# A first layer by seven products over two halves of 192 rows, in place of seven over 256 rows and four over 128

## The chip, the cores and the metric

The kernel runs on one core of one Trainium2 chip. The metric is device time in microseconds (us): the median of the runs, which is 640.2 us for the kernel before (three runs, 640.17, 640.20 and 640.79 us). A profile is one execution as the hardware profiler recorded it. Engines are called by their short names: PE (TensorE, the matrix engine), PEld (its weight loads), DVE (VectorE), ACT (ScalarE), POOL (GpSimd) and SP (SyncE, which issues most DMAs).

## What is computed

A recurrent attention block ("delta net") is followed by a two-layer network with an exact GELU. All is fp32.

```python
# q, k, v: (4 batches, 8 heads, 768 tokens, 48); beta: (4, 8, 768)
k_n = k / (norm(k) + 1e-6);  state = 0
for t in range(768):
    y[t]  = q[t] @ state
    state = state + beta[t] * outer(k_n[t], v[t] - state.T @ k_n[t])
x = y as (3072 tokens, 384)                   # 384 = 8 heads x 48
h = x @ w_in                                  # w_in:  384 x 2048
out = (0.5 * h * (1 + erf(h / sqrt(2)))) @ w_out   # w_out: 2048 x 384
```

## The kernel before, in words

The 768 tokens of each batch are cut into 12 chunks of 64 (`c` = 0 to 11). A chunk holds 4 x 64 = 256 tokens in two tiles `a` = 0, 1 of 128 tokens. Each chunk goes through the attention part and then, while the next chunk's attention is worked on, through the two layers of the network. One such stretch is called a step here. Ten steps (`c` = 2 to 11) use the fast forms of the two layers; chunks 0 and 1 use plain products (`fc1`, `fc2`), which the change leaves alone.

**First layer, `c` > 1 (`part_of_layer`, L906).** The contraction of 384 rows is three blocks of 128. Blocks 0 and 1 are treated as the two halves of a 2 x 2 block product (two token tiles, two halves of the contraction, two halves of `w_in`'s 2048 columns) and done by Winograd's seven products P1 to P7 instead of eight. The weight sums are made once (`sum_of_w_in`, L869), the sums of x once a step (`mix_x`, L878). Block 2 is done plainly, by four more products R11, R12, R21, R22. That makes eleven, each done in two blocks `b` of four matmuls 128 x 128 x 128 (L916), so 88 matmuls a step. The first block's eleven parts come before the second's. PE adds up what can be added in PSUM (tiles psX, psY, psZ, psV); ACT copies partial results to `pu` in SBUF, DVE adds the rest (L939, L947, L958, L968), ACT applies the GELU (through the helper `keep`, L902) and leaves it in `G`.

**Second layer (`second_layer`, L1032).** It has seven products again, each of eight matmuls that move 192 columns (`product_`, L859). `two` starts them in the order 1, 5, 2, 6, 4, 7, 3, and `read2` adds the results up on DVE.

**Attention around it.** Small matmuls that use 64 (or 48, or 32) rows and 64 columns of PE's array, several of them side by side in its parts: `against_state` (psK, L667), `solve` (psU, L702), `use` and `update` (psY, L732 and L743), `grams` and `queries` (psG, L414), `join_run` (psJ, L593). They come in groups of 32 to 64. `turns` (L782) transposes a finished chunk's x (L788) and one ACT copy puts it into `xT`, the moving operand of the first layer.

**What sets the order.** A plan (`emit`, L1062) sorts all steps by a due time, written in units of one chunk. DVE keeps the order of the plan, and so do those ACT instructions that pass through `keep`. The layers' matmuls on PE are tied in a line one behind the other (`behind`, L888); an attention group that is passed to `together` (L623) stands directly behind the matmul traced before it. PSUM is all given out: pool `ps` has two tiles "mlp" and two "dn" of double size, pool `small` has one "z" and one "sq". A tile's next use waits until the reads of its last use are over.

In the trace each fp32 matmul is two MATMUL records: 88 matmuls a step in ten steps are 1760 records of L916. A transpose is one record.

Of the kernel before, what the change touches and what calls it, by code (L numbers as in the profile page):

```python
# [19 lines left out]
def kernel(  # L20
# [301 lines left out]
    def sum_of_squares(u, h):  # L322

        if "both" not in ns:
            n23 = wk.tile([128, 2 * NA, H], F32, tag="n23", name="n23", bufs=1)
            ns[2], ns[3] = n23[:, 0:NA], n23[:, NA:]
            ns["both"] = n23
        if h == 0:
            u.ksq = wk.tile([128, H, D], F32, tag="ksq", name="ksq", bufs=1)
        keep(nc.scalar.activation, u.ksq[:, h], u.Kn[:, h, 0:D], ACT.Square,  # L330
             accum_out=ns[u.c][:, u.a, h:h + 1])
# [27 lines left out]
    def root(x):  # L359

        shape = list(x.shape)
        s = wk.tile(shape, F32, tag="root", name="root", bufs=1)
        r = wk.tile(shape, F32, tag="root_r", name="root_r", bufs=1)
        nc.vector.tensor_scalar(s.bitcast(U32), x.bitcast(U32), 0.5, 532487669.0,
                                op0=ALU.mult, op1=ALU.add)
        nc.vector.tensor_scalar_mul(x, x, 0.5)
        for i in range(3):
            nc.vector.reciprocal(r, s)
            nc.vector.tensor_tensor(r, r, x, op=ALU.mult)
            nc.vector.scalar_tensor_tensor(x if i == 2 else s, s, 0.5, r, ALU.mult, ALU.add)  # L370
# [204 lines left out]
    def join_run(g, ts0, ts1):  # L575
# [5 lines left out]
        for level, ts in enumerate((ts0, ts1)):  # L581
            if ts:
                if both is not None:
                    psJ = both[:, level]
                else:
                    psJ = small[0].tile([128, 512], F32, tag="sq" if level else "z", name="psJ")
                sets.append((level, ts[0] * H, psJ.rearrange("q (k n) -> q k n", n=2 * HB)))
# [120 lines left out]
    def solved(u, copy):  # L708
        u.U = wk.tile([128, H, D], F32, tag="U", name="U")
# [56 lines left out]
    def turn(u):  # L766
        if u.a == 0:
            xTs[u.c] = wk.tile([128, NM, NA * 128], F32, tag="xT", name="xT")
        xT = xTs[u.c]
        psX = sq("psX", NM, 128)  # L770
        for m in range(NM):
            cols = slice(m * 128, (m + 1) * 128)
            if u.c == 1:

                for i, part in enumerate((u.x, u.y)):
                    nc.tensor.matmul(psX[:, m, :], lhsT=part.rearrange("q h d -> q (h d)")[:, cols],
                                     rhs=ident, start=i == 0, stop=i == 1)
            else:
                nc.tensor.transpose(psX[:, m, :], u.x.rearrange("q h d -> q (h d)")[:, cols], ident)
        nc.scalar.copy(xT[:, :, u.a * 128:(u.a + 1) * 128], psX)  # L780

    def turns(us):  # L782
        c = us[0].c
        xT = xTs[c] = wk.tile([128, NM, NA * 128], F32, tag="xT", name="xT")
# [5 lines left out]
        keep(nc.scalar.copy, xT.rearrange("q m (a n) -> q a m n", n=128), psX)  # L790
# [73 lines left out]
    S1, L1 = {}, {}  # L864
# [10 lines left out]

    def of_x(c, k, a):
        return xTs[c][:, k, a * 128:(a + 1) * 128]

    def mix_x(c):
        t = more[0].tile([128, 3, 128], F32, tag="TX", name="TX")  # L880
        L1["T"] = {1: t[:, 0], 2: t[:, 1], 3: of_x(c, 0, 1), 4: t[:, 2]}
        for n, a, b in ((1, of_x(c, 0, 1), of_x(c, 0, 0)), (2, of_x(c, 1, 1), t[:, 0]),
                        (3, of_x(c, 1, 1), of_x(c, 0, 1)), (4, of_x(c, 1, 0), t[:, 1])):
            nc.vector.tensor_tensor(L1["T"][n], a, b, op=ALU.subtract)
# [21 lines left out]
    def part_of_layer(c, b, n):  # L906

        fs = slice(b * FB, (b + 1) * FB)

        def product(*args):  # L910
            behind(product_, *args)

        def product_(ps_, lhs, rhs, first):
            for i in range(FB):
                f = b * FB + i
                nc.tensor.matmul(ps_[:, i], lhsT=lhs[:, f // 2, f % 2 * 128:(f % 2 + 1) * 128],  # L916
                                 rhs=rhs, start=first and i == 0, stop=True,
                                 skip_group_check=not (first and i == 0))

        def half(k, a):  # L920
            return A[a][k][:, fs]

        def fresh(name, tag, pool):
            L1[name] = pool.tile([128, FB, 128], F32, tag=tag, name=f"ps{name}")
            return L1[name]

        if n == "P1":
            if b == 0:
                L1["pu"] = more[0].tile([128, 2, FB, 128], F32, tag="S1", name="pu")
            product(fresh("X1", "mlp", ps), block(0, 0), of_x(c, 0, 0), True)  # L930
            keep(nc.scalar.copy, L1["pu"][:, 0], L1["X1"])
        elif n == "P5":
            product(fresh("Z1", "z", small[0]), S1[1], L1["T"][1], True)
            keep(nc.scalar.copy, L1["pu"][:, 1], L1["Z1"])
            if b > 0:
                keep(nc.scalar.activation, L1["last"], L1["last"], ACT.Gelu)
        elif n == "P6":
            product(fresh("Y1", "mlp", ps), S1[2], L1["T"][2], True)
            nc.vector.tensor_tensor(L1["Y1"], L1["Y1"], L1["pu"][:, 0], op=ALU.add)  # L939
        elif n == "P2":  # L940
            product(L1["X1"], block(0, 1), of_x(c, 1, 0), False)
        elif n == "R11":
            product(L1["X1"], block(0, 2), of_x(c, 2, 0), False)
            keep(nc.scalar.activation, half(0, 0), L1["X1"], ACT.Gelu)
        elif n == "P7":
            product(L1["Y1"], S1[3], L1["T"][3], False)
            nc.vector.tensor_tensor(half(1, 1), L1["Y1"], L1["pu"][:, 0], op=ALU.add)  # L947
            keep(nc.scalar.activation, half(1, 1), half(1, 1), ACT.Gelu)
        elif n == "R22":
            product(L1["Z1"], block(1, 2), of_x(c, 2, 1), False)  # L950
            keep(nc.scalar.copy, L1["pu"][:, 0], L1["Z1"])
        elif n == "P3":
            product(fresh("V1", "sq", small[0]), S1[4], of_x(c, 1, 1), True)
        elif n == "R12":
            product(L1["V1"], block(0, 2), of_x(c, 2, 1), False)
        elif n == "P4":
            product(L1["Y1"], block(1, 1), L1["T"][4], False)
            nc.vector.tensor_tensor(half(0, 1), L1["V1"], L1["pu"][:, 1], op=ALU.add)  # L958
        else:
            product(L1["Y1"], block(1, 2), of_x(c, 2, 0), False)  # L960
            keep(nc.scalar.activation, half(1, 0), L1["Y1"], ACT.Gelu)
            L1["last"] = half(0, 1)
            if b == NB - 1:
                keep(nc.scalar.activation, L1["last"], L1["last"], ACT.Gelu)
                mix(c, 1, 1)

    def add_p5():
        nc.vector.tensor_tensor(L1["pu"][:, 1], L1["Y1"], L1["pu"][:, 1], op=ALU.add)  # L968
# [14 lines left out]
    def two(c, n):  # L983
        if n == 1:
            W2["X"] = ps.tile([128, 2, DH], F32, tag="mlp", name="psX2")
            W2["o"] = [wk.tile([128, DM], F32, tag="o_sb", name="o_sb") for a in range(NA)]
            product(W2["X"][:, 0], A[0][0], B11, True)
        elif n == 5:
            W2["Z"] = small[0].tile([128, DH], F32, tag="z", name="psZ2")
            product(W2["Z"], W2["S"], T[1], True)  # L990
            W2["p1"] = more[0].tile([128, DH], F32, tag="p1", name="p1")
            nc.scalar.copy(W2["p1"], W2["X"][:, 0])
# [9 lines left out]
        else:  # L1002
            W2["V"] = dn("psV2")[:, 0, 0:DH]
            product(W2["V"], A[0][1], B22, True)

    def read2(c, n):
        o, X, Y, Z = W2["o"], W2["X"], W2["Y"], W2["Z"]
        if n == 6:
            W2["u2"] = o[0][:, DH:]
            nc.vector.tensor_tensor(W2["u2"], Y[:, 0], W2["p1"], op=ALU.add)  # L1010
        elif n == 7:
            W2["u3"] = W2["p1"]
            nc.vector.tensor_tensor(W2["u3"], Y[:, 0], W2["p1"], op=ALU.add)
            nc.vector.tensor_tensor(o[1][:, 0:DH], X[:, 1], W2["u3"], op=ALU.add)
            nc.vector.tensor_tensor(o[1][:, DH:], Z, W2["u3"], op=ALU.add)
            tiles[c, 1].o = o[1]
            send(tiles[c, 1])
            nc.vector.tensor_tensor(W2["u2"], Z, W2["u2"], op=ALU.add)
            tiles[c, 0].o = o[0]
        else:  # L1020
            nc.vector.tensor_tensor(o[0][:, DH:], W2["V"], W2["u2"], op=ALU.add)
# [10 lines left out]
    def second_layer(c, n):  # L1032

        two(c, n)
        if n == 1:
# [5 lines left out]
    def ffn_steps(c):  # L1041
        ones = [(1.3, fc1, c, f) for f in range(NF)]
        if c > 1:
            return [(0.88, part_of_layer, c, b, n) for b in range(NB)
                    for n in ("P1", "P5", "P6", "P2", "R22", "R11", "P7", "P3", "R12", "P4", "R21")] + [
                (2.6, second_layer, c, n) for n in (1, 5, 2, 6, 4, 7, 3)]
# [175 lines left out]
    plan += [at(c + 0.958, c + 0.959, [(1.0, mix_x, c)]) for c in range(2, NC)]  # L1222
# [35 lines left out]
    for c in range(2, NC):  # L1258
        for b in range(NB):
            t = c + 1.06 + 0.2576 * b  # L1260
            plan += [at(t, t + 0.001, [(1.0, add_p5)])]
        plan += [at(c + 1.42, c + 1.421, [(1.0, mix, c, 1, 0)]),
                 at(c + 1.94, c + 1.941, [(1.0, read_x, c)]),
# [71 lines left out]
```

## Time and profile before

| what | from the profile | 
|---|---|
| median of the runs | 640.2 us |
| the profiled execution: its span, first to last instruction (its own time; no other is shown for it) | 638.7 us |
| PE, busy | 618.4 us (97% of the span) |
| DVE, busy | 496.6 us (78%) |
| ACT, busy | 259.9 us (41%) |
| POOL, busy | 64.9 us (10%) |
| first layer, `c` > 1 (L916), matmul records | 1760, each 128 rows x 128 columns, moving 128 |
| second layer, `c` > 1 (L859), matmul records | 1120, moving 192 |

Busy time is the union of the records of an engine. PE's records overlap (one of L916 lasts 275 ns, and the next starts 112 ns after it), so the time that a group costs is read from the chain of work that ended last, or from the distance of the starts, and not from the mean of one. The chain is the list of pieces of work that follow one another up to the last instruction, each with its start and its length; a piece runs until the next one takes over, so a delay at the beginning of a group is part of that group's piece.

### The profile page before, as it was taken

Reading aid. Unit: us, or ns where it says so; the run is one execution under the profiler, and the core shown is the slowest. Engines: PE = TensorE matmul, PEld = TensorE weight load, DVE = VectorE, ACT = ScalarE, POOL = GpSimd, SP = SyncE. Lnnn points to the kernel's source line nnn. Section 1 sums busy time; section 2 is a strip of 40 time slices with the busy share of each in tenths; the row PEclk is TensorE's granted clock in tenths of the full one; section 3 lists DMA queues with packets and bytes.
Section 4 is the critical chain, followed back from the end, with each engine's and each line's share of the span. In section 5 each row is a group of like instructions: output and inputs, shape, how many; then the busy total and the mean of one; then the engine's idle time right before and its main releaser. Section 6 shows DMA issues by size and latency. Waiting matters only on the chain.

```text
span 638.7 us, 22156 instructions
## 1 busy us (share of the span) xinstructions
PE 618.4 (97%) x9702; PEld 573.8 (90%) x9702; DVE 496.6 (78%) x1011; ACT 259.9 (41%) x586; POOL 64.9 (10%) x58
## 2 busy tenths in 40 slices
PE   6779999999999999999999999999999999999997
PEld 5667776776899999999999999999999999999997
DVE  6999989999799987999677999577999565354342
ACT  3576877624541265132265132265142253231230
POOL 4044002100300012001012001012001000000000
PEclk9977999999999999999999999999999999999999
DMA  9794884303442234221335222311222300100101
GB/s 134 172 280 139 149 175 137 50 1 73 73 67 44 47 51 77 56 36 36 58 48 79 54 27 47 57 27 28 52 29 38 62 4 2 26 2 3 26 2 25
DMA packets 158433, 39.79 MB, mean 62 GB/s; under 512 B 150016, under 2 KB 153216, under 8 KB 158336
## 3 DMA queue, kind: packets, MB, share of 16 engines
q1 hardware_dynamic: 155664, 37.34, 30.2%
q8 instruction: 76, 1.25, 0.8%
q10 hardware_dynamic: 2672, 1.03, 0.8%
q14 instruction: 21, 0.17, 0.1%
HBM read 33.62 MB, written 4.72 MB: 60 GB/s over the span
## 4 chain that ended last, share of the span: by engine, by line
PE 81%; DVE 11%; ACT 2%; DMA 2%; issue 2%; POOL 0%; SPq 0%; DVEq 0%; ACTq 0%; POOLq 0%
PE psX L859 12%; PE psY L916 11%; PE psX L916 8%; PE psY L859 8%; PE psV L916 5%; PE psZ L916 5%; PE psG L414 5%; PE psZ L859 4%; PE psV L859 4%; PE psK L667 3%; PE psO L829 3%; PE psJ L593 2%; DVE tmp L501 2%; DVE Nu L503 2%; PE psH L811 2%; PE psY L732 2%
## 5 line engine op out<-in xcount | busy, mean ns | idle before, releaser
L916 PE MATMUL psX<-xT,w_in_sb 128*128 128x128 f32 x480 | 64.5, 277 | 0.0
L503 DVE TENSOR_TENSOR Nu<-Nu,tmp 128x58 f32<-128x58 f32 (+13 forms) x168 | 58.5, 348 | 5.8
L501 DVE TENSOR_TENSOR tmp<-Nu 128x58 f32<-128x58 f32 (+13 forms) x168 | 59.2, 352 | 4.4
L916 PEld LDWEIGHTS psX<-xT,w_in_sb 128*128 128x128 f32 x480 | 58.8, 192 | 1.2 <-issue 0.3
L902 ACT COPY xT<-psX 128x768 f32<-128x768 f32 x9 | 7.2, 799 | 124.3 <-PE psX L788 124.3
L351 POOL TENSOR_TENSOR n<-n,half 128x16 f32<-128x16 f32 x10 | 30.2, 3020 | 247.2 <-DVE n L349 197.4
L859 PE MATMUL psX<-w_out_sb,G 128*128 128x192 f32 x320 | 55.3, 326 | 0.0
L859 PEld LDWEIGHTS psX<-w_out_sb,G 128*128 128x128 f32 x320 | 52.1, 190 | 0.0
L811 PE MATMUL psH<-xT,w_in_sb 128*128 128x256 f32 x192 | 44.4, 384 | 1.5 <-ACT G L902 1.3
L829 PE MATMUL psO<-w_out_sb,G 128*128 128x384 f32 x128 | 43.9, 490 | 0.0
L811 PEld LDWEIGHTS psH<-xT,w_in_sb 128*128 128x128 f32 x192 | 35.7, 190 | 8.8 <-ACT G L902 2.2
L916 PE MATMUL psY<-xT,w_in_sb 128*128 128x128 f32 x320 | 42.3, 275 | 0.0
L902 ACT COPY pu<-psZ 128x512 f32<-128x512 f32 x40 | 23.5, 587 | 39.5 <-PE psZ L916 39.5
L916 PEld LDWEIGHTS psY<-xT,w_in_sb 128*128 128x128 f32 x320 | 38.9, 192 | 0.0
L829 PEld LDWEIGHTS psO<-w_out_sb,G 128*128 128x128 f32 x128 | 23.6, 190 | 14.0
L902 ACT ACTIVATE G<-G 128x512 f32<-128x512 f32 x40 | 25.2, 629 | 20.5 <-DVE G L947 19.8
L376 POOL TENSOR_TENSOR V<-V,n 128x384 f32<-128x384 f32 x18 | 17.2, 965 | 135.3 <-DMA V<-in_v_dram 131.1
L939 DVE TENSOR_TENSOR psY<-psY,pu 128x512 f32<-128x512 f32 x20 | 14.0, 699 | 20.5 <-PE psY L916 18.7
L859 PE MATMUL psZ<-T,pu 128*128 128x192 f32 x160 | 28.6, 332 | 0.0
L859 PE MATMUL psY<-T,G 128*128 128x192 f32 x160 | 28.6, 332 | 0.0
L859 PE MATMUL psV<-w_out_sb,G 128*128 128x192 f32 x160 | 27.7, 326 | 0.0
L859 PE MATMUL psX<-T,G 128*128 128x192 f32 x160 | 27.6, 326 | 0.0
(183 smaller groups left out, 1349.7 us busy)
## 6 DMA issues: line engine op xcount, KB each, us to landing
Kp<-in_k_dram SPq DMA_DIRECT2D x76, 96.0 KB, 3.1
w_out_sb<-in_moe_w_in_dram SPq DMA_DIRECT2D x24, 256.0 KB, 4.1
w_raw<-in_moe_w_out_dram SPq DMA_DIRECT2D x16, 384.0 KB, 4.8
V<-in_v_dram SPq DMA_DIRECT2D x48, 96.0 KB, 3.1
out_dram<-o_sb SPq DMA_DIRECT2D x40, 96.0 KB, 2.2
Qp<-in_q_dram SPq DMA_DIRECT2D x64, 32.0 KB, 2.1
Qp<-in_q_dram SPq DMA_DIRECT2D x16, 96.0 KB, 4.4
Qp<-in_k_dram SPq DMA_DIRECT2D x32, 32.0 KB, 2.2
```

Of the source, the lines that this page charges most:

```text
L351: nc.gpsimd.tensor_tensor(flat, flat, half, op=ALU.pow)
L376: engine.tensor_tensor(u.V, u.V, ns[u.c][:, u.a].unsqueeze(2).to_broadcast([128, H, D]), op=ALU.mult)
L414: nc.tensor.matmul(psG[HALF[p], r, i * NP + j, :], lhsT=u.Kt[rows, p, j, :], rhs=(u.Qt if x else u.Kt)[rows, p, j, :], start=True, stop=True)
L501: nc.vector.tensor_tensor(tmp, nu[:, j + 1:, j:j + 1].to_broadcast([128, n, j]), nu[:, j:j + 1, 0:j].to_broadcast([128, n, j]), op=ALU.mult)
L503: nc.vector.tensor_tensor(nu[:, j + 1:, 0:j], nu[:, j + 1:, 0:j], tmp, op=ALU.add)
L667: nc.tensor.matmul(u.psK[to, x, r, j, :], lhsT=(u.Qt if x else u.Kt)[rows, p, j, :], rhs=St[rows, u.a, p ^ r, j, :], start=True, stop=True)
L811: nc.tensor.matmul(psH, lhsT=w_in_sb[:, f // 2, m, f % 2 * 128:(f % 2 + 1) * 128], rhs=xTs[c][:, m, :], start=(m == 0), stop=(m == NM - 1))
L829: nc.tensor.matmul(u.psO, lhsT=G[:, u.a, f, :], rhs=w_out_sb[:, f, :], start=(f == 0), stop=(f == NF - 1))
L859: nc.tensor.matmul(ps_, lhsT=lhs[:, f, :], rhs=rhs[:, f, :], start=first and f == 0, stop=f == FH - 1, skip_group_check=not first)
L902: i = fn(*args, **kw)
L916: nc.tensor.matmul(ps_[:, i], lhsT=lhs[:, f // 2, f % 2 * 128:(f % 2 + 1) * 128], rhs=rhs, start=first and i == 0, stop=True, skip_group_c ...
L939: nc.vector.tensor_tensor(L1["Y1"], L1["Y1"], L1["pu"][:, 0], op=ALU.add)
```

## The change

The contraction is cut into two halves of 192 rows, and all of the layer is done by the seven products. Half 0 is block 0 with rows 0 to 63 of block 2, half 1 is block 1 with rows 64 to 127 of block 2. So a product is a part with 128 rows (`wide`, four matmuls a block) and a part with 64 rows. The 64-row parts of two products are done together (`narrow`), one on rows 0 to 63 of PE's array and one on rows 64 to 127, matmul by matmul in turns; both use all 128 columns, and write to different PSUM tiles. The list `RUNS` has seven such pairs. A step is now seven times: two wide parts (four matmuls each), then a narrow run (eight matmuls). That is 56 matmuls with 128 rows and 56 with 64 rows, the latter in 28 pairs. Both blocks `b` are worked on in turns.

For this, block 2 of `w_in` is spread over both halves of the partitions once, by eleven ACT copies of 64 partitions x 512 (`spread_third`), and its sums made by six POOL additions of 128 x 512 (`sums_of_third`). `turns` writes x's third block twice, so that the one ACT copy becomes five. `mix_x` works on twice the elements, in two parts. The reads of PSUM become six copies, six additions and eight GELUs a step, in place of six copies, eight additions and eight GELUs. The second layer's first product moves ahead of the last wide part; its PSUM tile comes from "z" instead of "mlp", that of product 5 from "sq" instead of "z", that of product 3 from "mlp" instead of "dn"; the last psJ of a join comes from "mlp" instead of "sq". `xT` has one buffer instead of two, and `u.U` takes the place of `u.W`.

```diff
     def turns(us):
         ...
-        keep(nc.scalar.copy, xT.rearrange("q m (a n) -> q a m n", n=128), psX)
+        xT = xT.rearrange("q m (a n) -> q a m n", n=128)
+        keep(nc.scalar.copy, xT[:, :, 0:2], psX[:, :, 0:2])
+        for e in range(2):
+            for p in range(2):
+                keep(nc.scalar.copy, xT[HALF[p], :, 2 + e], psX[HALF[e], :, 2])
...
+    def spread_third(step):
+        ...
+        for dst, to, src, at_ in moves[step]:
+            keep(nc.scalar.copy, dst[to], src[at_])
+
+    def sums_of_third():
+        W3.update({1: natural(0, 0), 2: natural(0, 1), 4: natural(1, 1), 7: natural(1, 0)})
+        put = nc.gpsimd.tensor_tensor
+        put(W3[3], W3[3], W3[5], op=ALU.add)
+        ...
     def of_x(c, k, a):
-        return xTs[c][:, k, a * 128:(a + 1) * 128]
+        return xTs[c].rearrange("q (s k) n -> q s k n", k=2)[:, :, k, a * 128:(a + 1) * 128]
...
-    def part_of_layer(c, b, n):
-        ...
+    RUNS = [((1, 0), (2, 0)), ((5, 0), (1, 1)), ((6, 0), (3, 0)), ((6, 1), (2, 1)),
+            ((5, 1), (7, 0)), ((7, 1), (3, 1)), ((4, 0), (4, 1))]
...
+    def bank(n, b):
+        name = {1: "Y", 6: "Y", 7: "Y", 4: "Y", 5: "Z", 3: "Z", 2: "X"}[n] + str(b)
+        if n in (1, 5, 2):
+            pool, tag = {1: (ps, "mlp"), 5: (small[0], "z"), 2: (small[0], "sq")}[n]
+            L1[name] = pool.tile([128, FB, 128], F32, tag=tag, name="ps" + name)
+        return L1[name]
+
+    def wide(c, n, b):
+        def run():
+            ps_, (lhs, rhs) = bank(n, b), operands(c, n)
+            for i in range(FB):
+                ...
+                nc.tensor.matmul(ps_[:, i], lhsT=lhs[:, f // 2, f % 2 * 128:(f % 2 + 1) * 128],
+                                 rhs=rhs[:, 0], start=first, stop=True, skip_group_check=not first)
+        behind(run)
+
+    def narrow(c, *run_):
+        def run():
+            for i in range(FB):
+                for n, b in run_:
+                    rows = HALF[1 - b if n in (2, 3) else b]
+                    nc.tensor.matmul(L1[...][:, i],
+                                     lhsT=W3[n][rows, i // 2, i % 2 * 128:(i % 2 + 1) * 128],
+                                     rhs=operands(c, n)[1][rows, 1], start=False, stop=True,
+                                     skip_group_check=True)
+        behind(together, (run,))
+
+    def first_layer(c, r):
+        ...
+        narrow(c, *RUNS[r])
+        if r == 0:
+            copy(half(0, 0, 0), L1["Y0"])
+        elif r == 1:
+            copy(pu[:, 0], L1["Z0"])
+            copy(half(0, 0, 1), L1["Y1"])
+            add(0, 0, 0, L1["X0"])
+        ...
+        elif r == 5:
+            gelu(1, 1, 0)
+            add(0, 1, 1, L1["Z1"])
+            add(1, 1, 1, L1["Y1"], pu[:, 1])
+            gelu(0, 1, 1)
+            gelu(1, 1, 1)
+            mix(c, 1, 0)
         else:
+            gelu(1, 0, 0, L1["Y0"])
+            gelu(1, 0, 1, L1["Y1"])
...
     def two(c, n):
         if n == 1:
-            W2["X"] = ps.tile([128, 2, DH], F32, tag="mlp", name="psX2")
+            W2["X"] = small[0].tile([128, 2, DH], F32, tag="z", name="psX2")
...
+            steps = []
+            for r, (a, b) in enumerate(RUNS):
+                steps += [(0.88, wide, c, *a)] + [(2.6, second_layer, c, 1)] * (r == 6)
+                steps += [(0.88, wide, c, *b), (0.88, first_layer, c, r)]
+                steps += [(0.0, mix, c, 1, 1)] * (r == 6)
+            return steps + [(2.6, second_layer, c, n) for n in (5, 2, 6, 4, 7, 3)]
...
+    plan += [at(t, t + 0.001, [(1.0, spread_third, n)])
+             for n, t in enumerate((2.05, 2.12, 2.19, 2.62, 2.64))]
+    plan += [at(2.66, 2.661, [(1.0, sums_of_third)])]
```

## The prediction

> **What bounds the kernel now.** I read the page's totals first, then the busy time by stage, then the chain of work that ended last inside one step. The page:
>
> ```profile
> PE 618.4 (97%) x9702; PEld 573.8 (90%) x9702; DVE 496.6 (78%) x1011; ACT 259.9 (41%) x586; POOL 64.9 (10%) x58
> PE   6779999999999999999999999999999999999997
> PEclk9977999999999999999999999999999999999999
> ```
>
> PE is busy nearly all the time, at full clock after the first tenth. Busy time alone doesn't say that PE is the limit, since a matmul that waits for its engine can look busy. So I look at two stretches of the table by windows, one step with attention beside it and one of the last, without:
>
> ```profile
> 383.00:433.00 50.00, 50.00 (x905) 48.72 (x904) 38.85 (x77) 18.39 (x36) 5.45 (x3) 1.00 0.24 42
> 574.00:616.00 42.00, 42.00 (x488) 41.41 (x488) 17.07 (x33) 11.45 (x23) 0.00 (x0) 1.00 0.04 11
> ```
>
> The columns are the window, its length, then busy us and records of PE, PEld, DVE, ACT and POOL, the granted clock, the DMA share and GB/s. PE is busy without a gap; DVE has 11 us of 50 to spare, ACT 31. The chain shows what PE's time consists of (start, length, what):
>
> ```profile
> 193.23 1.08 PE psU L702 x64
> 194.31 0.95 PE psG L414 x64
> 195.25 2.80 PE psZ L859 x16
> 198.05 2.60 PE psX L859 x16
> ...
> 329.79 1.09 PE psX L916 x8
> 330.88 0.89 PE psY L916 x8
> 331.77 1.79 PE psV L916 x16
> 333.56 2.01 PE psK L667 x128
> 335.57 1.98 PE psY L916 x16
> 337.55 2.60 PE psX L859 x16
> 340.15 1.08 PE psU L702 x64
> 341.23 1.08 PE psJ L593 x32
> 342.31 1.09 PE psG L414 x64
> 343.40 2.80 PE psZ L859 x16
> ```
>
> Piece follows piece with nothing between, so from about 139 us, where the chain leaves DVE's elimination for PE, whatever is added to or taken from PE's work goes into the end. Three prices can be read here.
>
> - Eight records of L916 (four matmuls) take 0.89 us in a row: 0.112 us each.
> - The same eight take 1.09 us when the group before them used 64 rows (329.79). Likewise 16 of L859 take 2.80 instead of 2.60. So it costs PE 0.20 us to go from a group of small matmuls to 128 rows.
> - psG takes 0.95 us behind psU, which also uses 64-row parts, and 1.09 behind psJ, which uses 32-row parts; both use 64 columns. So it costs 0.14 us to enter a group whose number of rows differs, from small to small too. psK agrees: in its middle four records side by side start every 0.058 us (spacing of the starts in the trace), so 128 records should take 1.87 us, and the piece is 2.01.
>
> **The change part by part: matmuls.** The layer is now 22 parts of four matmuls a step (11 parts, two blocks): 22 x 0.893 = 19.65 us. Afterwards it is 14 wide parts, 14 x 0.893 = 12.50 us, and seven narrow runs of eight matmuls each. If the two 64-row matmuls of a pair run side by side, a run is eight pairs of records at one spacing. No record here has 64 rows and 128 columns. The nearest are these: L916, 0.112 us for the same 128 columns moved; psJ's run of 32, which goes two by two (in its middle 0.0587 us a pair for 64 moved columns), twice that 0.117; and, if the halves don't overlap, 0.223. psK and psY (L732) run four side by side, among them two that share their columns and differ in rows, as the new pairs do; so I take overlap, and 0.112, since psJ's small excess looks like a fixed amount rather than a share. A run is 0.896 us, seven 6.27. Matmuls: 12.50 + 6.27 - 19.65 = -0.88 us a step, **-8.8 us** in ten steps. (With 0.117 it would be -6.0; with 0.223, +53.)
>
> **The change of rows.** Every narrow run is a group of 64 rows between groups of 128. In the order in which the changed program is built, the 70 runs (7 x 10) are left 52 times to a 128-row matmul, 14 times to psK, psU or psG, 4 times to psJ. An exit to 128 rows is the row above: 1.09 - 0.893 = 0.197 us. An entry to a narrow run is not in the trace: 0.14 at the low end (64 weight columns), 0.20 at the high end (the entry to 128 rows, which loads 128 columns of weights, as the narrow run does); zero below both, if it is row counts with fewer columns alone that cost, for which psG behind psJ gives no support. I take 0.197, as the narrow run's weights are as wide. An attention group directly behind a narrow run pays its 0.14 as it does now behind a wide one, so there only the run's entry is new. Sum: 70 x 0.197 + 52 x 0.197 = 24.0 us; one narrow run stands behind psG, which saves that group's exit, so **+23.8 us**. (At 0.14 an entry it is 19.8.)
>
> Here the Trainium skill has a rule, "TensorEngine Tiling (Array Packing)", section Tiling Modes, Key Properties: a change of the tiling mode drains TensorE. It speaks against the change and gives no price. The trace agrees, and charges more than a drain: 64 weight columns cost 0.14 and 128 cost 0.197, so by a straight line 0.083 is fixed and the rest grows with the load of the weights. By a drain of 0.083 alone, the 122 changes cost 10.1 us and the sum is +1.3; by the rows it is +15.0. The same page's Theoretical Speedup (up to 2x where 64 rows are contracted) alone gives -8.8.
>
> **What the other engines do.** The changes of order put none of it in front of PE, by these covers.
>
> - The second layer's first product waits for "z", thus for DVE's addition of Z1 after the sixth narrow run. Between them stands one wide part: 0.89 + 0.20 = 1.09 us. The last record lasts 0.275 us, DVE starts about 0.11 us later (as L939 does now), and the addition takes 0.69 (L939: 0.70), together 1.08. It just fits if DVE is free; behind one of its 0.4 us additions (L501, L503) PE, and all that is queued on it, waits up to 0.4. In the steps in which psK stands between, 2 us more cover it. Bounds: 0 and 10 x 0.4 = 4 us.
> - psJ's last part waits for the GELU of Y0 (0.60 us, ACT); psU's 0.97 us stands between. The other reads have at least three PE pieces (about 2.9 us) until their tile is used again, against 0.7 us on DVE or 0.6 on ACT.
> - `turns`: one copy of 0.80 us becomes one of 0.59 (as pu's, 128 x 512) and four smaller of at most 0.4, 2.2 us; product 3 (2.60 us) lies over it, and the first wide part needs the first copy alone. `read_x` and `mix_x` queue behind these; their first reader on PE comes 2.7 us after product 3. If DVE, waiting 2.2 us for the copies, fell behind by 1.4 a step, its spare 11 us would take it. Without these covers it is 0 to 1.4 us a step.
> - DVE has two additions less (-1.4 us) and about 0.6 us more in `mix_x`.
> - Once, before the first fast step: eleven ACT copies (at most 0.59 each, 6.5 us) at 110 to 150 us, where ACT is busy 9.4 us of 30 after 120 us; six POOL additions (0.97 us for 128 x 384 now, so about 1.3 each, 7.7 us), after which POOL's `prep` and the scaling of V are queued. The first narrow run comes at about 167 us, POOL would be done by 160. To 139 us the chain is DVE's elimination, which has none of this in front. Bounds: 0 to 1.5 us.
> - SP's and ACT's DMA issues keep their places; no bytes are added, and the wider spacing of steps gives loads more time. `u.U` in `u.W` and one `xT` buffer wait for reads that ended a dozen us before: nothing.
>
> I take 0.5 us for all these waits; the bounds together are 0 and about 10.
>
> **Sum.** -8.8 + 23.8 + 0.5 = +15.5 us. Against the profiled execution's 638.7 us this makes a span of 654.2; the runs' median stood 1.5 us above that span, so 640.2 + 15.5 = **655.7 us**.
>
> **The rivals.**
>
> - **Faster: 64 rows with all 128 columns change nothing.** If PE is slowed only when the columns are cut too, entry and exit of the narrow runs are free and -8.8 remains: about 631 us. The place is the 122 changes; the sign turns where one costs 8.8 / 122 = 0.072 us. For it: every costly change in the fast steps involves 64-column groups. Against it: psJ to psG changes rows alone, and costs 0.14. Chance 0.10.
> - **Only the fixed part is paid**, the weights being loaded during it: +1.3 us, 641 to 646 with other waits. For it: loads are hidden inside a run. Against it: 1.09 and 2.80 in the rows above, at 128 columns. Chance 0.08.
> - **DVE or ACT come late**: the tight "z" wait and the five copies cost 5 to 11 us more, 661 to 667. For it: 1.08 against 1.09, and DVE's 39 us of 50. Against it: PE's longer step leaves DVE more room. Chance 0.12.
> - **The pairs don't overlap**: +53 instead of -8.8, about 718 us. For it: no pair in the trace has 128 columns each. Against it: psK's four in 0.058 us. Chance 0.05.
> - **As summed**, 650 to 661: chance 0.65.
>
> **How the numbers follow.** The prediction is the likeliest case. The range has to leave out no more than 0.2: I leave out the faster case, the unpaired one and some of the drain case's lower part, and go from 643 to 667. About 0.2% (1.3 us) is what a measurement tells from no change; the drain case at its lower end falls there, 0.02. Faster is 0.10, slower 0.88.
>
> **What would show it.** In the changed chain, each narrow run's 16 records should take about 1.1 us, the wide part behind it 1.09 instead of 0.89, the second wide part 0.89; psK and psU behind a narrow run stay at 2.01 and 1.08. PE should stay free of gaps; a gap ahead of the second layer's first product, released by DVE, would be the "z" wait. Narrow runs of 0.9 us followed by 0.89 would prove the faster rival, runs of 1.8 or more the unpaired one. Most likely to make the number wrong is the entry price, which I took from its nearest neighbour.

## The result

The changed kernel takes 657.48 us (median of four runs, 656.76 to 657.83) against 640.5 us for the kernel before in the same series (640.17 to 640.93): 1.0264 times as long, 95% interval 1.025 to 1.0279. The forecast was 655.7 us, slower. The profiled execution has a span of 655.0 us, against 638.7 before and 654.2 forecast.

The page after, the same lines as before:

```profile
PE 634.1 (97%) x10182; PEld 575.2 (88%) x10182; DVE 488.4 (75%) x991; ACT 280.3 (43%) x651; POOL 76.0 (12%) x64
PE   6779999999999999999999999999999999999997
PEclk9976999999999999999999999999999999999999
```

PE is still busy all the time and has more to do; DVE has less (496.6 before), ACT and POOL more. By windows, a step with attention and one without (window, length, then busy us and records of PE, PEld, DVE, ACT, POOL, then clock, DMA share and GB/s):

```profile
400.00:450.00 50.00, 50.00 (x967) 47.24 (x967) 34.78 (x71) 20.91 (x43) 6.85 (x3) 1.00 0.24 42
590.00:635.00 45.00, 45.00 (x553) 42.82 (x550) 17.27 (x33) 13.07 (x29) 0.00 (x0) 1.00 0.04 10
```

There are no gaps, as before, and the clock is full. The chain of work that ended last shows where the time is (start, length, what; L978 are the wide parts, L988 the narrow runs, L668 is psK, L703 psU, L876 the second layer):

```profile
344.49 0.89 PE psY L978 x8
345.38 1.09 PE psY L988 x16
346.47 1.08 PE psU L703 x64
...
368.38 0.89 PE psY L978 x8
369.27 0.89 PE psX L978 x8
370.17 0.30 PE psY L988
...
371.26 1.09 PE psZ L978 x8
372.35 0.89 PE psY L978 x8
...
383.55 2.01 PE psK L668 x128
385.56 1.09 PE psY L978 x8
```

A narrow run of 16 records takes 1.09 us, where eight spacings would be 0.89. (Most runs stand in the chain as 16 small pieces, since their two PSUM tiles alternate; that of 370.17 lasts until 371.26, where the next wide part takes over, 1.09 as well.) The wide part behind a run takes 1.09, the second 0.89. psK and psU behind a run take 2.01 and 1.08, as they did behind wide parts. What PE waited for in all its work from 165 us on is little (engine, tile and line; whom it waited for; us, times, longest):

```profile
PE psJ L594 <- ACT G L950: 0.4, 1, 0.4
PE psY L978 <- DVE o_sb L1085: 0.4, 1, 0.4
```

So from the first layer's first record to PE's last, 469.1 us have become 484.7 (from the starts of the records), +15.6, of which less than 1 us is waiting.

### The profile page after: what moved, and what is told of

It is laid out like the page before. It is cut to its first block, busy times and chain, and to the rows that moved or that the text cites. A ratio compares the mean times of both kernels' runs of the same rounds, so it can differ in the third digit from the quotient of the medians.

```text
span 655.0 us, 23138 instructions
## 1 busy us (share of the span) xinstructions
PE 634.1 (97%) x10182; PEld 575.2 (88%) x10182; DVE 488.4 (75%) x991; ACT 280.3 (43%) x651; POOL 76.0 (12%) x64
## 4 chain that ended last, share of the span: by engine, by line
PE 78%; DVE 11%; ACT 5%; issue 2%; DMA 2%; ACTq 0%; SPq 0%; DVEq 0%
PE psY L978 11%; PE psX L876 10%; PE psY L876 7%; PE psY L988 7%; PE psZ L978 6%; PE psG L414 4%; PE psZ L876 4%; PE psH L828 3%; PE psV L876 3%; PE psO L846 3%; PE psK L668 3%; PE psZ L988 3%; PE psX L978 2%; PE psJ L594 2%; PE psT L393 2%
## 5 line engine op out<-in xcount | busy, mean ns | idle before, releaser
L950 ACT COPY xT<-psX 64x256 f32<-64x256 f32 (+1 forms) x45 | 17.5, 410 | 103.6 <-PE psX L801 103.1
L351 POOL TENSOR_TENSOR n<-n,half 128x16 f32<-128x16 f32 x10 | 32.6, 3258 | 215.0 <-DVE n L349 165.2
L876 PE MATMUL psX<-w_out_sb,G 128*128 128x192 f32 x320 | 55.9, 328 | 0.0
L876 PEld LDWEIGHTS psX<-w_out_sb,G 128*128 128x128 f32 x320 | 52.0, 190 | 0.2
L950 ACT COPY G<-psY 128x512 f32<-128x512 f32 x40 | 23.5, 588 | 60.6 <-PE psX L988 43.8
L828 PE MATMUL psH<-xT,w_in_sb 128*128 128x256 f32 x192 | 46.4, 394 | 0.5 <-ACT o_sb L850 0.4
L988 PE MATMUL psY<-xT,w_in_sb 64*128 64x128 f32 x320 | 46.2, 285 | 0.0
L828 PEld LDWEIGHTS psH<-xT,w_in_sb 128*128 128x128 f32 x192 | 36.6, 196 | 8.9 <-ACT G L834 1.8
L950 ACT ACTIVATE G<-G 128x512 f32<-128x512 f32 x60 | 37.3, 632 | 15.8 <-DVE G L1008 15.5
L978 PE MATMUL psY<-xT,w_in_sb 128*128 128x128 f32 x320 | 43.4, 279 | 0.4 <-DVE o_sb L1085 0.4
L978 PEld LDWEIGHTS psY<-xT,w_in_sb 128*128 128x128 f32 x320 | 39.4, 192 | 1.6 <-issue 0.6
L988 PEld LDWEIGHTS psY<-xT,w_in_sb 64*128 64x128 f32 x320 | 38.6, 187 | 2.4
L1008 DVE TENSOR_TENSOR G<-psZ,G 128x512 f32<-128x512 f32 x20 | 13.8, 691 | 34.1 <-ACT G L950 21.8
L876 PE MATMUL psZ<-T,pu 128*128 128x192 f32 x160 | 28.7, 332 | 0.0
L876 PE MATMUL psY<-T,G 128*128 128x192 f32 x160 | 28.6, 332 | 0.0
L876 PE MATMUL psV<-w_out_sb,G 128*128 128x192 f32 x160 | 27.7, 326 | 0.0
L876 PE MATMUL psX<-T,G 128*128 128x192 f32 x160 | 27.6, 326 | 0.0
```

Source lines behind the costliest of these rows:

```text
L351: nc.gpsimd.tensor_tensor(flat, flat, half, op=ALU.pow)
L828: nc.tensor.matmul(psH, lhsT=w_in_sb[:, f // 2, m, f % 2 * 128:(f % 2 + 1) * 128], rhs=xTs[c][:, m, :], start=(m == 0), stop=(m == NM - 1))
L876: nc.tensor.matmul(ps_, lhsT=lhs[:, f, :], rhs=rhs[:, f, :], start=first and f == 0, stop=f == FH - 1, skip_group_check=not first)
L950: i = fn(*args, **kw)
L988: nc.tensor.matmul(L1[{1: "Y", 6: "Y", 7: "Y", 4: "Y", 5: "Z", 3: "Z", 2: "X"}[n] + str(b)][:, i], lhsT=W3[n][rows, i // 2, i % 2 * 128:(i ...
```

## The experiments

The theory was that PE's change between groups of 128 and of 64 rows costs about 0.2 us each way, and that the narrow pairs themselves run as fast as hoped. The rivals: the pairs run slowly; or the time goes into the reads, the five copies of `turns` or new waits. The ratios are to runs of the kernel before on the same chip, in the same series; it took 640.0 to 640.5 us in every series, so differences to the changed kernel's 657.48 us are taken across series.

**The change of rows by itself, in the kernel before (e7).**

```diff
+                if n[0] == "R":
+                    nc.tensor.matmul(ps_[:, i], lhsT=lhs[0:64, f // 2, f % 2 * 128:(f % 2 + 1) * 128],
+                                     rhs=rhs[0:64], start=False, stop=True, skip_group_check=True)
+                    continue
```

> The kernel before, with the four products of the third block on rows 0 to 63 alone: as many matmuls, records, reads and waits as before, the order unchanged, but half of the third block is left out, and PE changes from 128 rows to 64 and back at each of these groups. It measures the disputed cost by itself. In the built order 69 such groups stand; 55 are left to a 128-row matmul and 14 to an attention group, and 10 stand behind an attention group, whose exit is saved. Theory: 69 x 0.197 + 55 x 0.197 - 10 x 0.197 = 22.5 us more, about 663 us. Rival (the change of rows is cheap, and the changed kernel loses its time by its pairs, its copies or its waits): 640 to 645 us.

Measured: 661.51 us against 640.01, ratio 1.0332 (1.0316 to 1.0349): +21.5 us where 22.5 were expected. The chain of this kernel (L917 are the groups with 64 rows, L920 the others of the first layer):

```profile
375.12 0.89 PE psX L917 x8
376.01 1.09 PE psY L920 x8
...
380.16 1.08 PE psY L917 x8
381.25 1.09 PE psX L920 x8
382.34 0.89 PE psZ L920 x8
383.23 0.89 PE psY L920 x8
384.12 0.89 PE psX L920 x8
385.02 1.09 PE psZ L917 x8
386.10 2.01 PE psK L667 x128
```

The kernel has as many matmuls as the one before and does less arithmetic; eight records take 1.09 wherever the number of rows has just changed, 0.89 elsewhere. The group at 375.12 is the second of two with 64 rows in a row and takes 0.89, so the matmuls with 64 rows are not slower themselves. There are no pairs, no new copies and no new waits in it. This alone is enough to settle the cause; the rival that the change of rows is cheap falls.

**The change without the 64-row matmuls (e1).**

```diff
-                for n, b in run_:
-                    rows = HALF[1 - b if n in (2, 3) else b]
+                n, b = run_[i % 2]
...
-                                     lhsT=W3[n][rows, i // 2, i % 2 * 128:(i % 2 + 1) * 128],
-                                     rhs=operands(c, n)[1][rows, 1], start=False, stop=True,
+                                 lhsT=W3[n][:, i // 2, i % 2 * 128:(i % 2 + 1) * 128],
+                                 rhs=operands(c, n)[1][:, 1], start=False, stop=True,
```

> Each pair of 64-row matmuls is replaced by one matmul with all 128 rows into one of the pair's two PSUM tiles (the two in turns), so half of the third block's sums are left out and the rest is summed over both halves; the number of streaming slots, the reads, the copies and the order stay. Theory (the loss is the change of rows at entry and exit of a run): the 122 changes at 0.197 us go, 23.8 us, so 657.5 becomes about 633.7 us, 1% faster than the kernel before. Rival (the loss is in the reads, the five copies of turns, or the new waits for PSUM tiles): these all stay, so it stays above 650 us. A narrow run's piece in the chain should fall from 1.09 to 0.89 us, and the wide part behind it likewise.

Measured: 639.55 us against 640.4, ratio 0.9991 (0.9976 to 1.0007). That is 17.9 us below the changed kernel, not 23.8: 5.9 us more than expected. The waits of PE from 165 us on:

```profile
PE psZ L978 <- DVE G L1007: 1.9, 2, 1.0
PE psG L414 <- issue: 1.1, 1, 1.1
PE psY L978 <- DVE o_sb L1084: 0.5, 1, 0.5
PE psK L668 <- issue: 0.4, 1, 0.4
```

3.9 us, against 0.8 in the changed kernel. By the distance of the record starts beyond their usual spacing it is 5.2 against 1.0, and the first layer begins 0.7 us later, so about 4.9 of the missing 5.9 us are found. Without the changes of rows PE is faster, and some of what it gains goes to new waits: the wide part that begins Z1 waits for DVE's addition of Z0 in the first two steps, in which DVE has least to spare. The larger part of the loss is gone with the changes of rows, so the rival that keeps it in reads and copies falls. But without any price of rows, this order of work took as long as the kernel before, and not the 8.8 us less that the matmuls alone were counted for.

**Fewer changes (e2).**

```diff
-            for r, (a, b) in enumerate(RUNS):
-                ...
+            for group in ((0, 1), (2, 3), (4,), (5,), (6,)):
+                for r in group:
+                    a, b = RUNS[r] if r != 4 else RUNS[r][::-1]
+                    steps += [(0.88, wide, c, *a)] + [(2.6, second_layer, c, 1)] * (r == 6)
+                    steps += [(0.88, wide, c, *b)]
+                for r in group:
+                    steps += [(0.88, first_layer, c, r)]
+                ...
```

> Runs 0 and 1, and runs 2 and 3, are put behind one another: eight wide parts' worth of matmuls in a row, then two narrow runs in a row, so that a step has five groups of 64 rows instead of seven, with the same matmuls and the same reads. Theory (a price per entry and exit): 20 entries and 20 exits less in ten steps, 20 x 0.394 = 7.9 us, so about 649.6 us, plus at most 2 us for ACT's copies that now have less time before their tile is used again. Rival (the price is paid per 64-row matmul, since pairs run slower than one 128-row matmul): no change, 657.5 us.

(A run has two wide parts, so it is four wide parts in a row, not eight. The edit also lets the two wide parts of run 4 change places.)

Measured: 651.17 us, ratio 1.0168 (1.0153 to 1.0184): 6.3 us below the changed kernel, inside what was expected (7.9, less up to 2 for waits). PE's listed waits are 2.6 us against 0.8, the longest 1.1 for an ACT copy ahead of a wide part. With as many pairs and fewer entries the time falls, so the price is paid per entry and exit, not per matmul.

**Narrower weights (e3), and both together (e5).**

```diff
-                for n, b in run_:
+                for (n, b), h in ((run_[0], 0), (run_[1], 1), (run_[0], 1), (run_[1], 0)):
                     rows = HALF[1 - b if n in (2, 3) else b]
-                    nc.tensor.matmul(L1[...][:, i],
-                                     lhsT=W3[n][rows, i // 2, i % 2 * 128:(i % 2 + 1) * 128],
+                    f0 = i % 2 * 128 + h * 64
+                    nc.tensor.matmul(L1[...][HALF[h], i],
+                                     lhsT=W3[n][rows, i // 2, f0:f0 + 64],
```

> Each 64-row matmul with 128 weight columns becomes two with 64 weight columns, so four stand side by side on rows x columns, as in the attention groups; the same multiplications in twice the matmuls. Theory (the part of the price above the fixed one is the load of the weights that no matmul hides, so it goes with the weight columns): entries cost 0.14 instead of 0.197, 70 x 0.055 = 3.9 us, and the 14 attention groups of 64 rows directly behind a run are entered without a change, 14 x 0.146 = 2.0 us: about 651.6 us, if four records start at the same spacing of 0.112 us as two did. Rival (each record costs its own issue time of 0.007 us on top): 8 x 70 x 0.013 us more, about 659 us. Second rival (128 columns cost no more than 64): only the 2.0 us, 655.5 us.

Measured: 657.11 us, ratio 1.0263 (1.0242 to 1.0284), the same as the changed kernel. Piece by piece the theory held: by the record starts a run takes 1.034 us instead of 1.091, the 0.057 that lie between 0.197 and 0.14, and psK directly behind a run starts 0.090 us after the run's last record, where it was 0.201 to 0.202. So rows alone do not decide: psK (64 rows, 64 columns) paid behind a run of 64 rows and 128 columns, and pays nothing there when the columns agree too. What costs here is a change of the shape, in rows or in columns. The gain is eaten by waits that the changed kernel does not have, in the middle of attention groups:

```profile
PE psG L414 <- issue: 3.5, 4, 1.7
PE psK L668 <- issue: 0.5, 1, 0.5
PE psZ L978 <- DVE G L1009: 0.4, 1, 0.4
```

"issue" says that the profile shows nothing that PE waited for. Piece by piece against the changed kernel, by the starts in the two profiled runs (e3's is the slowest of its four), psG and psK cost 5.2 us more, the runs and psU 6.1 us less. Another 1.5 us are lost in the two wide parts behind the longest wait, where the granted clock was about half. More on both below. The first rival of this run, that each record costs its issue time, is wrong, since four records of different parts start within 0.020 us and the next four come at the old spacing; the second, that 64 columns are entered no cheaper than 128, is wrong by the 0.057.

> Both earlier edits together: five groups of 64 rows a step instead of seven, and each 64-row matmul split into two of 64 weight columns. Theory (entries and exits have a price, the entry's goes with the weight columns, and an attention group of 64 rows behind a run has none): 50 runs enter at 0.14 instead of 0.197, 2.9 us less, and 14 attention groups are entered for nothing, 2.0 us less, so about 646 us on the side of PE's work; since splitting alone brought 0.4 us where 5.9 were due, with 5.6 us of waits inside attention groups and ahead of wide parts, the same waits would make it 650 us. If it is as fast as batching alone (651) or slower, splitting brings nothing whatever its entries cost.

Measured: 652.94 us (four runs, 651.57 to 657.89), ratio 1.0214 (1.0162 to 1.0265), not distinguishable from batching alone (1.0168, 1.0153 to 1.0184). The split does not pay here even where there are fewer runs; 3.4 us of waits of the "issue" kind in psG are there too.

**Do the pairs overlap? (e4, e6).**

```diff
-            for i in range(FB):
-                for n, b in run_:
+            for n, b in run_:
+                for i in range(FB):
```

> The matmuls of a run in another order: first the four of one product, then the four of the other, so that neighbours use the same 64 rows and can't run side by side. Nothing else changes. Theory (the pairs overlap fully): a run takes 16 records at 0.112 us instead of 8 spacings, 0.89 us more, 70 runs: 62.5 us, about 720 us. Rival (the pairs gain little from standing side by side, and the loss against the kernel before is that): below 680 us.

Measured: 694.08 us, ratio 1.0838 (1.0816 to 1.0859), 36.6 us above the changed kernel, between the two expectations. The timeline of PE shows why (start, length, engine, line, what):

```profile
384.78 0.82 PE L988 MATMUL psY<-xT,w_in_sb 64*128 64x128 f32 x5
385.33 0.37 PE L988 MATMUL psX<-xT,w_in_sb 64*128 64x128 f32 x1
385.44 0.27 PE L988 MATMUL psY<-xT,w_in_sb 64*128 64x128 f32 x1
385.55 0.27 PE L988 MATMUL psX<-xT,w_in_sb 64*128 64x128 f32 x1
385.55 0.27 PE L988 MATMUL psY<-xT,w_in_sb 64*128 64x128 f32 x1
385.66 0.27 PE L988 MATMUL psX<-xT,w_in_sb 64*128 64x128 f32 x1
385.66 0.27 PE L988 MATMUL psY<-xT,w_in_sb 64*128 64x128 f32 x1
385.77 0.72 PE L988 MATMUL psX<-xT,w_in_sb 64*128 64x128 f32 x5
```

In the program all eight records of psY come before the first of psX. On PE the first of psX starts at 385.33, together with the fifth of psY. Where both halves of the rows are at work the pair takes one spacing, 0.11 us; where psY or psX is alone, a record takes as long as a pair does. So a run has 12 spacings instead of 8 or 16, 4 x 0.112 = 0.45 us more, and psX's first weights are a second load that nothing hides, 0.1 us. From a run's first record to the first one behind it, it is 1.640 us against 1.091; 70 x 0.549 = 38.4 us, close to the 36.6 measured. The pairs of the changed kernel overlap fully. PE finds an overlap by itself too, but here only from the point where four records of the first product were left.

```diff
-            for i in range(FB):
-                for n, b in run_:
+            for n, b, i in [(*x, i) for j in (0, 2) for x in run_ for i in (j, j + 1)]:
                 ...
```

> The matmuls of a run in the order two of the first product, two of the second, two of the first, two of the second. In the run with four and four the second product's first record started together with the first product's fifth, so four records of the other half were still ahead of it. Theory (PE starts a matmul on the free half of the rows up to four records ahead of its place): here the second product starts together with the first, pairs overlap fully, 657.5 us. Rival (the halves overlap only at the seam between two products, by chance of the load's timing): two seams of partial overlap, a run of about 1.3 us, 670 us or more.

Measured: 664.61 us, ratio 1.0381 (1.0357 to 1.0404), 7.1 us above the changed kernel. Neither number came. The pair does start together, as the theory said (383.39 and 383.40 in the timeline), but once in each run a record is late by about a spacing, here one of psX:

```profile
383.39 0.37 PE L987 MATMUL psY<-TX,W 64*128 64x128 f32 x1
383.40 0.37 PE L987 MATMUL psX<-xT,w_in_sb 64*128 64x128 f32 x1
...
383.95 0.37 PE L987 MATMUL psX<-xT,w_in_sb 64*128 64x128 f32 x1
384.05 0.27 PE L987 MATMUL psY<-TX,W 64*128 64x128 f32 x1
384.16 0.27 PE L987 MATMUL psX<-xT,w_in_sb 64*128 64x128 f32 x1
```

The record at 383.95 lasts 0.37 instead of 0.27 us, as the first ones of a run do, whose weights nothing hides. By the record starts a run takes 1.193 us instead of 1.091; 0.102 us in each of 70 runs is 7.1 us, which is the loss. Why the weights of just this record come late is not settled.

None of these versions is faster than the kernel before.

## Why the prediction was right, point by point

- **Matmuls, -8.8 us.** Right. The spacing of the narrow pairs is 0.105 us to the first of the next pair after 0.007 within it, so 0.112, the value taken among 0.112, 0.117 and 0.223; e4 shows that without overlap it would be double.
- **The change of rows, +23.8 us.** Right, and the only term that decides the sign. The run's piece of 1.09 less 0.896 gives 0.194 for the entry, where 0.197 was taken from its neighbour and 0.14 was the other end; the exit is 0.197. e7 measured the sum by itself, 21.5 us where this count gives 22.5. Of the straight line (0.083 fixed, and 0.057 for each 64 weight columns) e3 confirms the 0.057 between 64 and 128 columns; the 0.083 is where the line ends at no columns, which no run measured. At 0.194 to 0.197 a change, a drain of 0.083 alone, which would have made +1.3 us, is not what PE pays here.
- **The waits, +0.5 us.** 0.8 us listed. Half of it is psJ's wait for a GELU, once, which the prediction had as covered by psU. The tight wait for "z" cost next to nothing: in the six steps without psK in between, DVE's addition ended 0.11 us before the second layer's first product began, and that product's piece is 2.64 instead of 2.60 us. DVE's busy time fell by 8.2 us (8 were expected), and the four small copies of `turns` take 0.37 us each (0.4 was the bound).
- **Sum.** PE's stretch came out at +15.6 us where 15.5 was the whole. That it is so close is partly luck: the entries cost 0.2 us less than taken (70 x 0.003), the waits some 0.3 us more. The span has 0.7 us more: the first layer begins 0.2 us later, and 0.5 us is at the end, which no step of the prediction had; it took ACT's DMA issues to keep their places. There ACT's last copy stands behind two DMA issues of its own queue, which wait for DVE:

```profile
648.83 0.37 DVE o_sb L1088
...
649.22 0.47 ACTq L840
...
649.72 0.61 ACTq L840
...
650.51 0.32 ACT o_sb L950
```

  The median moved by 17.0 us and the profiled spans by 16.3, since the profiled run is the lowest of its four; the forecast of 655.7 is 1.8 us below the median.
- **POOL's sums** took 9.6 us (four of 1.3 and two of 2.2) instead of 7.7, under the same cover. A mis-sized term that cost nothing.
- **The rivals.** The faster case, that rows alone cost nothing as long as the columns are whole, is shown wrong by e7. e1 speaks against its 631 us too: without the price of rows the same order came to 639.55, with 5.2 us of waits for DVE and inside attention groups.

## What to carry to other kernels

Splitting a contraction so that a part of it uses half of PE's rows can pay only if the half-row matmuls stand in long groups or beside others of the same shape, and two runs in a row (e2) were not long enough here: each entry and exit costs about 0.2 us here, nearly as much as two matmul records of 128 columns (0.224). It could be read before the change from a profile that has small and large matmuls side by side, as the excess of the first piece behind a change. Count the groups before the matmuls: here 280 pairs saved 8.8 us and 122 changes cost 24. Neighbours that are to run side by side belong matmul by matmul in turns; even two by two lost 0.1 us in each run.

## What the runs showed of the hardware that was not expected

- PE does not start matmuls strictly in program order where they use different halves of its rows: in e4 a matmul of the other half started together with one that stands four records ahead of it. The Trainium skill, "TensorE: Matmul & The Clock Gate", Part 3, says that matmuls start and end strictly in program order; for matmuls on different halves these runs decide otherwise.
- The waits called "issue" inside attention groups are at a fixed place of the instruction stream. Counting PE's records (loads, matmuls and its semaphore instructions) from the start of the program, each such stop of over 0.5 us from one start to the next inside psG or psK, seven in e1 and e3, four in e5 and one in e2, ends before a record whose index leaves 193 when divided by 256. The instruction queue (q8) moves packets of 16384 bytes, one for about 256 of PE's records: 76 for 19510 in the kernel before, 80 for 20474 in the changed one, 88 for 22714 in e3. Each of the twelve stops ended 1.2 to 1.6 us after the packet of its number had ended (the 42nd for index 42 x 256 + 193). Nowhere in these nine kernels, from 60 us on, does a record at such an index start less than 1.2 us behind its packet; the median distance is 4.6 to 5.8 us. So at these stops the instructions had come late: the stream ran dry. That small matmuls are the reason, since they use up many instructions in a short time, fits e3 and e5, which have 11302 matmul records against 10182 and the most of it, but was not tried by itself.
- Behind two of these stops the granted clock fell. In e5, in the profiled run, PE stood 1.02 us in psG up to 350.4 us, and for the three microseconds from 352 on the granted clock was 0.52; in e3 it stood 1.68 us up to 238.2 us, and the clock was 0.51 behind it (the last three columns are clock, DMA share and GB/s; the first line is e5's, the second e3's):

```profile
352.00:355.00 3.00, 3.00 (x11) 3.00 (x11) 1.69 (x3) 0.00 (x0) 0.20 (x1) 0.52 0.35 46
238.20:241.70 3.50, 3.50 (x21) 3.38 (x21) 1.03 (x3) 2.99 (x7) 2.36 (x1) 0.51 0.39 48
```

  The second layer's product there took 4.48 us of e5's chain for 16 records instead of 2.80, and the two wide parts of e3 took 2.00 and 1.49 instead of 1.09 and 0.89. The length of the stop does not decide it alone: after stops of 1.07 us in psG, in e1 (up to 345.4 us) and in e5 (up to 252.7 us), the granted clock stayed at 1.00. What does is open.
